# Top-32 attention with a feed-forward block: the mask as a parametric ReLU on ScalarE, the mean taken from x

## The chip, the cores and the metric

One core of a Trainium2 chip runs the whole program. The metric is the device time of one execution in microseconds (us); a comparison goes by the median of some runs. A core has TensorE (PE; its weight loads are PEld), VectorE (DVE), ScalarE (ACT), GpSimd (POOL) and SyncE (SP), each with a queue of its own that is worked off in order. Waits between them go by semaphores.

## The reference

Inputs are q, k and v of 8 batches x 8 heads x 576 rows x 64, a gain of 512, and two weight matrices of 512 x 2048 and 2048 x 512 in float64.

```python
scores = scale * np.matmul(q, k.transpose(0, 1, 3, 2))
kth = np.partition(scores, -32, axis=-1)[..., -32:-31]
scores = np.where(scores >= kth, scores, -1e9)
scores = scores - np.max(scores, axis=-1, keepdims=True)
attn = np.exp(scores); attn = attn / (attn.sum(-1, keepdims=True) + 1e-09)
out = np.matmul(attn, v)                       # then (B,H,S,D) -> x of (B,S,H*D)
mu, var = mean(x), variance(x)                 # along a row of 512
xn = (x - mu) / np.sqrt(var + 1e-06) * g_ln
y = x + np.maximum(xn @ w_ch1, 0.0) @ w_ch2
```

So each row of scores keeps its 32 largest, and the result goes through a normalisation, a two-layer feed-forward and a sum.

## The kernel before, in words

**Units.** Attention is cut into 160 units. A whole unit is 128 query rows of a pair of heads (two tiles of 128 x 576 scores); a rest unit (32 of them) holds the last 64 rows of both heads in one tile. A job is a batch, a pair of heads and two or three units; a group is what shares one product with v. Batch 0 has jobs [0, 1], [2, 3] and the rests apart.

**Steps.** The program is written out by hand, in steps n. `scores` of unit n+1 (L345: matmuls, and copies from PSUM by ACT) and `select` of unit n (L379: four rounds of MAX8 with three MATCH_REPLACE8 a tile, on VectorE, that find the 32nd largest value `thr` and the largest, `top`) stand in step n. In step n+1 POOL masks (`prepare`, `mask`, L398 and L412): it writes -1e30 where a score is below `thr` and adds the scores. In step n+2 ACT takes the exponentials (`weigh`, L422) with their sum, and TensorE turns them (`turn`, L441). In step n+3, after a group's last unit, `values` multiplies by v and `place` turns the result back and writes it to x, divided by the sums (`put`, L518). Sums of a group are inverted by `reciprocal` on VectorE. For the first 16 units (`shared`) ACT does half of the mask, with Sign and Relu, and POOL subtracts.

**Weights.** The float64 weights come in 32 pieces of 128 x 512 (`Piece`), two a step, batches 0 to 15. `fetch` loads a piece a step ahead; `split` takes size, low word and sign apart on ACT (Abs, Copy, Sign; L170 to L174) and limits the size on POOL (L175); a step later `shift` moves its bits on VectorE (L178) and `join` adds and signs it on POOL (L184, L185). For w_ch1, once four pieces of a column block are there, `mean_of` has TensorE take the mean over rows, weighted with the gain (L216), and `centre` on VectorE multiplies by the gain and subtracts (L227). So the mean of x never has to be taken from x.

**Feed-forward.** `Block` (L555) holds two or three row tiles of x. `stats` gives mean and variance on VectorE (L569), `std` the square root on ACT (L573), `inverse` the reciprocal. `items` lists its TensorE work with costs: `turn_x`, `hidden` (matmul with w1, then Relu on ACT, L619) and `project` (matmul with w2; at the end ACT scales with `rstd`, L633, POOL adds x, L634, and SP stores). `give` puts a block's items on the list `todo` at a step that is counted from its last unit (L709). `fill` stands eight times in a step and takes items off the list, as many as the planner's share allows: 1.2 us a call while weights are not all there, later an eighth of VectorE's planned cost of the unit (10.3 or 5.3 us) less TensorE's own (`slot`, L766). An item with a condition (`may`) holds up those behind it: `hidden` needs its columns centred, `project` its piece joined, the last one the block's `inverse`.

**Buffers.** Scores have 4 buffers, exponentials 3, raw weights and x share 4, PSUM has 5 of a short kind and 3 for products.

Of the kernel before, what the change touches and what calls it, by code (L numbers as in the profile page):

```python
# [18 lines left out]
MASKED = -1.0e30  # L19
LN_EPS = 1.0e-6  # L20
J = 4
# [7 lines left out]
def kernel(  # L29
# [9 lines left out]
):  # L39

# [48 lines left out]
    scpool = pool("sc", 4)  # L89
    wpool = pool("wk", 2)  # L90
    epool = pool("e", 3)
# [40 lines left out]
    class Piece:  # L132
# [26 lines left out]
        def split(self):  # L159
            def tmp(name, dt):  # L160
                return hpool.tile([P, DM], dt, tag="h", name=name)

            high = self.raw[:, :, 1].bitcast(FP32)
            self.size = tmp("size", U32)
            self.low = tmp("low", FP32)

            pl, tag = ((opool, "o"), (rpool, "r"))[self.i % 2]
            self.sign = pl.tile([P, DM], FP32, tag=tag, name="sign")
            size_f = self.size[:].bitcast(FP32)
            nc.scalar.activation(size_f, high, AF.Abs)  # L170
            nc.scalar.activation(
                self.low[:], self.raw[:, :, 0], AF.Copy, bias=2.0, scale=2.0**-51
            )
            nc.scalar.activation(self.sign[:], high, AF.Sign)  # L174
            nc.gpsimd.tensor_scalar(size_f, size_f, HIGH_MAX, HIGH_MIN, ALU.min, ALU.max)  # L175
# [6 lines left out]
        def join(self):  # L182
            size = self.size[:]
            nc.gpsimd.tensor_tensor(size, size, self.low[:].bitcast(U32), ALU.add)  # L184
            nc.gpsimd.tensor_tensor(  # L185
                self.dst, size.bitcast(FP32), self.sign[:], ALU.mult
            )
            ready[self.i] = now[0]
# [4 lines left out]
    centred = [None] * (DFF // DM)  # L193
    pieces = [Piece(i) for i in range(2 * NF)]
    gmat = [None]
    means = {}

    grow = hpool.tile([NC, P], FP32, tag="h", name="grow")

    def load_gain():  # L200
        ps = turned()
        nc.tensor.transpose(ps[:, 0:NC], grow[:], ident[0:NC, 0:NC])
        nc.scalar.copy(gcol[:], ps[:, 0:NC])
        ones = hpool.tile([P, P], FP32, tag="h", name="ones")
        nc.gpsimd.memset(ones[:], 1.0)
        gmat[0] = hpool.tile([P, NC, P], FP32, tag="h", name="gmat")
        for c in range(NC):
            nc.gpsimd.tensor_scalar(
                gmat[0][:, c], ones[:], gcol[:, c : c + 1], 1.0 / DM, ALU.mult, ALU.mult
            )  # L210

    def mean_of(nb):

        means[nb] = product("mean")
        for c in range(NC):
            nc.tensor.matmul(  # L216
                means[nb][:],
                gmat[0][:, c],
                w1[:, c, nb * DM : (nb + 1) * DM],
                start=(c == 0),  # L220
                stop=(c == NC - 1),
            )

    def centre(nb):
        for c in range(NC):
            w = w1[:, c, nb * DM : (nb + 1) * DM]
            nc.vector.scalar_tensor_tensor(  # L227
                out=w, in0=w, scalar=gcol[:, c : c + 1], in1=means[nb][:],
                op0=ALU.mult, op1=ALU.subtract,
            )  # L230
        centred[nb] = now[0]
# [4 lines left out]
    for n in range(-1, 2 * NF):  # L236
        size = 0 if n < 0 else 2
        batches[n], queue = queue[:size], queue[size:]

    def weights(n, phase):  # L240

        now, before = batches.get(n, []), batches.get(n - 1, [])
        if phase == 0:
            for x in batches.get(n + 1, []):
                x.fetch()
            for x in before:
                x.shift()
            for x in now[0::2]:
                x.split()
        elif phase == 1:  # L250
            for x in before:
                x.join()
            for x in now[1::2]:
                x.split()
            for x in batches.get(n - 2, []):
                if x.i < NF and x.c == NC - 1:
                    mean_of(x.i // NC)
        elif phase == 2:
            for nb in means:
                if centred[nb] is None:  # L260
                    centre(nb)
# [67 lines left out]
    class Unit:  # L329
        def __init__(self, job, group, qt):  # L330
            self.job, self.group, self.qt = job, group, qt
            self.rest = qt == J
            self.tiles = [(0, 1)] if self.rest else [(0,), (1,)]
            self.shared = False
# [63 lines left out]
    def prepare(u):  # L398

        nt = len(u.tiles)  # L400
        u.bias = small.tile([P, 2], FP32, tag="bias", name="bias")
        u.e = epool.tile([P, 2, S], FP32, tag="e", name="e")
        if u.shared:
            u.less = small.tile([P, 1], FP32, tag="less", name="less")
            nc.scalar.mul(u.less[:], u.thr[:, 0, 7:8], -1.0)
            nc.scalar.mul(u.bias[:, 0:nt], u.top[:, 0:nt, 0], -scale)
            nc.scalar.activation(u.e[:, 0], u.sc[:, 0], AF.Sign, bias=u.less[:])
            nc.scalar.activation(u.e[:, 0], u.e[:, 0], AF.Relu, scale=MASKED)
        else:
            nc.gpsimd.tensor_scalar_mul(u.bias[:, 0:nt], u.top[:, 0:nt, 0], -scale)  # L410

    def mask(u, t):  # L412
        e, sc = u.e[:, t], u.sc[:, t]
        if u.shared and t == 0:
            nc.gpsimd.tensor_tensor(e, sc, e, ALU.subtract)
        else:
            nc.gpsimd.tensor_scalar(  # L417
                e, sc, u.thr[:, t, 7:8], MASKED, ALU.is_lt, ALU.mult
            )
            nc.gpsimd.tensor_tensor(e, e, sc, ALU.add)  # L420

    def weigh(u, t):  # L422
        g = u.group
        if g.den is None:
# [3 lines left out]
            u.e[:, t], u.e[:, t], AF.Exp, bias=u.bias[:, t : t + 1], scale=scale,  # L428
# [126 lines left out]
    class Block:  # L555
# [7 lines left out]
        def stats(self, i):  # L563
# [6 lines left out]
            nc.vector.bn_aggr(out=self.mv[:, i, :], in_=st[:])  # L570

# [10 lines left out]
        def items(self):  # L582
# [38 lines left out]
            def project(i, f):  # L621
# [9 lines left out]
                if f == NF - 1:  # L631
                    o = opool.tile([P, DM], FP32, tag="o", name="o")
                    nc.scalar.mul(o[:], ps["o"][:], self.rstd[:, i : i + 1])  # L633
                    nc.gpsimd.tensor_tensor(o[:], o[:], self.x[i], ALU.add)  # L634
                    for dst, rows in self.dsts[i]:
                        nc.sync.dma_start(dst, o[rows, :])
# [9 lines left out]
                        lambda f=f: done(centred[f * P // DM]),  # L646
# [45 lines left out]
    for u in units[: max(n for n in batches if batches[n]) + 1]:  # L692
        u.shared = True

# [11 lines left out]
    for j in jobs:  # L706
        if j.hp == NHP - 1:
            b = j.b
            step = j.last + 4  # L709
# [24 lines left out]
    for j in fresh[2:]:  # L734
# [6 lines left out]
    def pe_cost(n):  # L741
# [3 lines left out]
        if at(n - 2):  # L745
            c += 0.67 if at(n - 2).rest else 1.0
        u = at(n - 3)
        if u and u.group.last == n - 3:
            c += 3.0
# [22 lines left out]
    recips, rows_of = {}, {}  # L772

    def arrived(n, key, x):
        blk, i = block_of[key]
        blk.x[i] = x
        rows_of.setdefault(n + 1, []).append((blk, i))

    load(fresh[0], nc.sync, nc.scalar)
    weights(-1, 0)  # L780
    turn_heads(fresh[0])
    load(fresh[1], nc.sync, nc.scalar)
    nc.sync.dma_start(grow[:], g_ln.rearrange("(c p) -> c p", p=P))
    scores(units[0])
    turn_heads(fresh[1])
    load(fresh[2], nc.sync, nc.sync)
    for n in range(END):
# [4 lines left out]
        u, nxt, mk, ex = at(n), at(n + 1), at(n - 1), at(n - 2)  # L792
        g = at(n - 3).group if at(n - 3) and at(n - 3).group.last == n - 3 else None
        g = g if g and not g.quick else None
        late = at(n - 4)
# [3 lines left out]
        if ex:  # L799
            weigh(ex, 0)  # L800
        if nxt:
            scores(nxt)
        if n == 0:
            load_gain()
# [6 lines left out]
        if mk:  # L811

            prepare(mk)
            order = list(range(len(mk.tiles)))
            if mk.shared:
                order.reverse()
            mask(mk, order[0])
        weights(n, 0)
        fill()
# [3 lines left out]
        if parts:  # L823
            parts[0]()
        if ex and ex.rest:
            keep_den(ex)
# [7 lines left out]
        for blk, i in rows_of.pop(n, []):  # L834
            blk.stats(i)
        for blk in gives.get(n - 1, []):
            blk.std()
        if mk and len(mk.tiles) > 1:
            mask(mk, order[1])
        weights(n, 1)  # L840
        fill()
# [3 lines left out]
        if late:  # L845
            place_rest(late.job.b, late.job.hp)
        fill()
# [6 lines left out]
        if ex and ex.group.last == n - 2 and ex.group.sums is not None:  # L854
            recips.setdefault(n + 1, []).append(ex.group.sums)
        last_rest = at(n - 3)
# [4 lines left out]
        weights(n, 2)  # L861
# [3 lines left out]
        fill()  # L865
        if mk and mk.job.last == n - 1:
            load_values(mk.job)
        if ex and ex.group.quick and ex.group.last == n - 2:

            g = ex.group  # L870
            values(g)
            for den in recips.pop(n + 1):
                nc.vector.reciprocal(den, den)
            place(g)
        if u:
            select(u, 3)
        if g and g.job.hp == NHP - 1:
            for qt in g.qts:
                if qt < J:
                    arrived(n, (g.job.b, qt), xs[g.job.b, qt])  # L880
        if late and late.job.hp == NHP - 1:
            r = late.job.b // 2
            arrived(n, ("r", r), rs[r])
# [34 lines left out]
```

## Time and profile before

| | us |
|---|---|
| median of 3 runs | 1763.67 (1763.66 to 1764.48) |
| profiled execution | 1762.83 |
| its span, first to last instruction | 1760.9 |
| PE busy | 1651.3 (94%) |
| DVE busy | 1522.1 (86%) |
| POOL busy | 1196.2 (68%) |
| ACT busy | 983.8 (56%) |
| DMA | 66.7 MB, 38 GB/s on the mean |

Busy time is that of an engine in the span of the profiled execution. Matmuls overlap, and their ends are modelled, so a busy TensorE is judged by the distance of the starts. A group's row gives line, engine, operation, written and read tiles, shapes and count, then its busy time and the mean of one instruction in ns, then the idle time of the engine just before and who ended it. In the timeline a row is the start, the duration, and what ran; brackets hold the idle time before it.

### The profile page before, as it was taken

Reading aid. Unit: us, or ns where it says so; the run is one execution under the profiler, and the core shown is the slowest. Engines: PE = TensorE matmul, PEld = TensorE weight load, DVE = VectorE, ACT = ScalarE, POOL = GpSimd, SP = SyncE. Lnnn points to the kernel's source line nnn. Section 1 sums busy time; section 2 is a strip of 40 time slices with the busy share of each in tenths; the row PEclk is TensorE's granted clock in tenths of the full one; section 3 lists DMA queues with packets and bytes.
Section 4 is the critical chain, followed back from the end, with each engine's and each line's share of the span. In section 5 each row is a group of like instructions: output and inputs, shape, how many; then the busy total and the mean of one; then the engine's idle time right before and its main releaser. Section 6 shows DMA issues by size and latency. Waiting matters only on the chain.

```text
span 1760.9 us, 23686 instructions
## 1 busy us (share of the span) xinstructions
PE 1651.3 (94%) x7433; PEld 1005.2 (57%) x7433; DVE 1522.1 (86%) x3160; ACT 983.8 (56%) x2621; POOL 1196.2 (68%) x882
## 2 busy tenths in 40 slices
PE   3668879999899999999999999999999999999998
PEld 1335446666555575655546666575555757575564
DVE  7998779999999999999999999999999999960000
ACT  5676856565655566557646656566555665561110
POOL 5886887777776787777777687687768868760000
PEclk9868899999999999999999999999999999999999
DMA  5432312101210022002111121012201210000000
GB/s 136 124 86 67 90 37 54 40 20 21 50 31 7 26 47 47 20 20 47 21 42 25 21 53 28 26 24 45 39 12 26 43 34 20 20 20 12 0 18 12
DMA packets 249348, 66.70 MB, mean 38 GB/s; under 512 B 240516, under 2 KB 240520, under 8 KB 249224
## 3 DMA queue, kind: packets, MB, share of 16 engines
q1 hardware_dynamic: 244488, 64.61, 16.2%
q10 hardware_dynamic: 4736, 0.59, 0.3%
q8 instruction: 59, 0.97, 0.2%
q14 instruction: 65, 0.53, 0.1%
HBM read 55.71 MB, written 9.44 MB: 37 GB/s over the span
## 4 chain that ended last, share of the span: by engine, by line
PE 45%; DVE 33%; issue 14%; POOL 5%; ACT 2%; DMA 1%; DVEq 0%; POOLq 0%; SPq 0%; ACTq 0%
DVE m L387 17%; PE hps L607 15%; PE ops L624 14%; DVE wk L392 13%; PE scps L370 6%; PE tp L451 4%; PE av L504 4%; POOL e L417 2%; PE av L511 1%; DVE size L178 1%; POOL e L420 1%; DVE qT L325 1%; DVE kT L325 1%; DVE w L227 1%; ACT e L427 1%
## 5 line engine op out<-in xcount | busy, mean ns | idle before, releaser
L417 POOL TENSOR_SCALAR e<-sc,m 128x576 f32<-128x576 f32 x272 | 604.1, 2221 | 208.9 <-DVE m L387 137.9
L387 DVE MAX8 m<-wk 128x8 f32<-128x576 f32 x864 | 612.6, 746 | 3.7
L607 PE MATMUL hps<-xT,w 128*128 128x256 f32 (+1 forms) x2048 | 545.0, 411 | 7.4 <-ACT xT L599 6.2
L624 PE MATMUL ops<-w,h 128*128 128x512 f32 x1152 | 542.2, 601 | 7.1 <-POOL w L185 7.1
L607 PEld LDWEIGHTS hps<-xT,w 128*128 128x128 f32 x2048 | 374.0, 191 | 113.7 <-issue 18.8
L392 DVE MATCH_REPLACE8 wk<-m,wk 128x576 f32<-128x576 f32 x576 | 423.8, 742 | 0.0
L420 POOL TENSOR_TENSOR e<-e,sc 128x576 f32<-128x576 f32 x272 | 383.4, 1410 | 22.7
L624 PEld LDWEIGHTS ops<-w,h 128*128 128x128 f32 x1152 | 202.6, 191 | 195.5 <-issue 180.4
L370 PE MATMUL scps<-kT,qT 64*128 64x288 f32 (+3 forms) x1344 | 236.4, 439 | 26.5 <-DVE qT L325 19.9
L351 ACT COPY sc<-scps 128x288 f32<-128x288 f32 x576 | 198.5, 417 | 91.4 <-PE scps L370 83.1
L451 PE MATMUL tp<-ident,e 128*128 128x128 f32 x1152 | 180.9, 281 | 56.1 <-ACT e L427 56.0
L427 ACT ACTIVATE e<-e,bias 128x576 f32<-128x576 f32 x288 | 227.4, 790 | 8.6 <-POOL e L420 4.0
L451 PEld LDWEIGHTS tp<-ident,e 128*128 128x128 f32 x1152 | 143.8, 144 | 144.8 <-ACT e L427 70.9
L370 PEld LDWEIGHTS scps<-kT,qT 64*128 64x128 f32 (+1 forms) x1344 | 134.6, 181 | 136.1 <-issue 49.1
L392 DVE MATCH_REPLACE8 wk<-m,sc 128x576 f32<-128x576 f32 x288 | 211.9, 742 | 0.0
L387 DVE MAX8 m<-sc 128x8 f32<-128x576 f32 x288 | 203.4, 743 | 9.2 <-ACT sc L351 9.1
L619 ACT ACTIVATE h<-hps 128x256 f32<-128x256 f32 (+1 forms) x256 | 104.8, 412 | 185.9 <-PE hps L607 185.0
L634 POOL TENSOR_TENSOR o<-o,x 128x512 f32<-128x512 f32 x32 | 40.7, 1271 | 245.8 <-ACT o L633 224.9
L463 ACT COPY pt<-tp 128x512 f32<-128x512 f32 x256 | 150.3, 587 | 90.0 <-PE tp L451 88.4
L504 PE MATMUL av<-pt,vb 128*64 128x256 f32 (+2 forms) x1088 | 146.0, 409 | 2.8 <-ACT pt L463 2.0
L504 PEld LDWEIGHTS av<-pt,vb 128*64 128x64 f32 x1088 | 72.5, 140 | 68.6 <-issue 24.5
L516 ACT COPY oT<-av 128x256 f32<-128x256 f32 (+2 forms) x68 | 26.2, 386 | 108.7 <-PE av L511 108.7
(71 smaller groups left out, 1038.6 us busy)
## 6 DMA issues: line engine op xcount, KB each, us to landing
vb<-in_v_dram SPq DMA_DIRECT2D x136, 128.0 KB, 2.4
raw<-in_moe_w_ch_dram SPq DMA_DIRECT2D x32, 512.0 KB, 4.2
kin<-in_k_dram SPq DMA_DIRECT2D x128, 72.0 KB, 2.4
qin<-in_q_dram SPq DMA_DIRECT2D x120, 72.0 KB, 2.5
out_dram<-o SPq DMA_DIRECT2D x32, 256.0 KB, 2.1
ends<-in_v_dram SPq DMA_DIRECT2D x136, 16.0 KB, 2.1
dr<-den SPq DMA_DIRECT2D x64, 0.2 KB, 1.7
out_dram<-o SPq DMA_DIRECT2D x8, 128.0 KB, 2.3
```

The source lines that it names most:

```text
L351: nc.scalar.copy(u.sc[:, t, s * HALF : (s + 1) * HALF], made[s][t][:, 0:HALF])
L370: nc.tensor.matmul(ps[i * R : i * R + ql, o : o + width], qT[r, q0 : q0 + ql], kT[r, k0 : k0 + width], start=True, stop=True,)
L387: nc.vector.max(m[:, t, :], u.cur[t])
L392: nc.vector.match_replace(u.wk[t][:], m[:, t, :], u.cur[t], LOWEST)
L417: nc.gpsimd.tensor_scalar(e, sc, u.thr[:, t, 7:8], MASKED, ALU.is_lt, ALU.mult)
L420: nc.gpsimd.tensor_tensor(e, e, sc, ALU.add)
L427: nc.scalar.activation(u.e[:, t], u.e[:, t], AF.Exp, bias=u.bias[:, t : t + 1], scale=scale, accum_out=g.den[:, col : col + 1],)
L451: nc.tensor.transpose(ps[:, c * P : (c + 1) * P], u.e[:, t, c * P + t * R : (c + 1) * P + t * R], ident[:],)
L463: nc.scalar.copy(g.pt[:, t * J : (t + 1) * J, q0 : q0 + P], ps[:].rearrange("p (c n) -> p c n", n=P),)
L504: nc.tensor.matmul(av[h * D : (h + 1) * D, 0 : g.nq], vb[:, h * J + c, :], g.pt[:, h * J + c, 0 : g.nq], start=(c == 0), stop=False,)
L607: nc.tensor.matmul(ps["h"][:, 0:N], w1[:, c, f * P : (f + 1) * P], xT[0][:, c, 0:N], start=(c == 0), stop=(c == NC - 1),)
L624: nc.tensor.matmul(ps["o"][:], hT[f][:, i * P : (i + 1) * P], w2[:, f, :], start=(f == 0), stop=(f == NF - 1),)
```

## The change

The mask is no longer made on POOL. ACT takes Prelu of `thr - score` with a slope of 2**-90: negative or zero (the kept scores) is scaled to almost nothing, positive stays. Exp then takes a scale of -scale * 2**90 and a bias of scale * (thr - top), which POOL computes for the unit; so kept scores give their exponential and the others zero. Both stand in `weigh`, one step after the selection; a unit's turning, values, placing and its block come a step earlier, too, and buffers of scores and exponentials fall to 3 and 2. The gain is multiplied in `join` on POOL; `mean_of` and `centre` go, and POOL subtracts the mean from x after `stats`, which now stands at the end of the step that placed x. The conversion of the output (Identity with a scale and a bias) adds the mean again. Odd pieces get their size by a product with the sign on POOL in place of Abs. Weights start a step earlier, the second job's k and q are turned in step 0, and a copy in front loads ACT's table.

```diff
-MASKED = -1.0e30
+SLOPE = 2.0**-90
-    scpool = pool("sc", 4)
+    scpool = pool("sc", 3)
-    epool = pool("e", 3)
+    epool = pool("e", 2)
             size_f = self.size[:].bitcast(FP32)
-            nc.scalar.activation(size_f, high, AF.Abs)
+            if self.i % 2 == 0:
+                nc.scalar.activation(size_f, high, AF.Abs)
...
+            if self.i % 2:
+                nc.gpsimd.tensor_tensor(size_f, high, self.sign[:], ALU.mult)
...
+            size = size.bitcast(FP32)
+            if self.i < NF:
+                nc.gpsimd.tensor_scalar_mul(size, size, gcol[:, self.c : self.c + 1])
+            nc.gpsimd.tensor_tensor(self.dst, size, self.sign[:], ALU.mult)
...
-    for n in range(-1, 2 * NF):
-        size = 0 if n < 0 else 2
-        batches[n], queue = queue[:size], queue[size:]
+    for n in range(-1, NF - 1):
+        batches[n], queue = queue[:2], queue[2:]
...
+        b = u.bias[:, 0:nt]
+        nc.gpsimd.tensor_tensor(b, u.thr[:, 0:nt, 7], u.top[:, 0:nt, 0], ALU.subtract)
+        nc.gpsimd.tensor_scalar_mul(b, b, scale)
-    def mask(u, t):
...
         nc.scalar.activation(
-            u.e[:, t], u.e[:, t], AF.Exp, bias=u.bias[:, t : t + 1], scale=scale,
+            u.e[:, t], u.sc[:, t], AF.Prelu, bias=u.thr[:, t, 7:8], scale=-1.0, alpha=SLOPE
+        )
+        nc.scalar.activation(
+            u.e[:, t], u.e[:, t], AF.Exp, bias=u.bias[:, t : t + 1], scale=-scale / SLOPE,
             accum_out=g.den[:, col : col + 1],
...
             nc.vector.bn_aggr(out=self.mv[:, i, :], in_=st[:])
+            nc.gpsimd.tensor_scalar_sub(x, x, self.mv[:, i, 0:1])
...
-                    nc.scalar.mul(o[:], ps["o"][:], self.rstd[:, i : i + 1])
+                    nc.scalar.activation(
+                        o[:], ps["o"][:], AF.Identity,
+                        bias=self.mv[:, i, 0:1], scale=self.rstd[:, i : i + 1],
+                    )
...
-                        lambda f=f: done(centred[f * P // DM]),
+                        lambda f=f, c=c: done(ready[f * P // DM * NC + c]),
...
-            step = j.last + 4
+            step = j.last + 3
...
-    for j in fresh[2:]:
+    for j in fresh[1:]:
...
     load(fresh[0], nc.sync, nc.scalar)
+    nc.scalar.copy(gcol[:, 0:1], eps[:])
+    for x in batches[-1]:
+        x.fetch()
+    turn_heads(fresh[0])
+    nc.sync.dma_start(grow[:], g_ln.rearrange("(c p) -> c p", p=P))
+    load(fresh[1], nc.sync, nc.scalar)
+    scores(units[0])
+    load_gain()
     weights(-1, 0)
-    turn_heads(fresh[0])
-    load(fresh[1], nc.sync, nc.scalar)
-    nc.sync.dma_start(grow[:], g_ln.rearrange("(c p) -> c p", p=P))
-    scores(units[0])
-    turn_heads(fresh[1])
-    load(fresh[2], nc.sync, nc.sync)
+    weights(-1, 1)
...
-        u, nxt, mk, ex = at(n), at(n + 1), at(n - 1), at(n - 2)
+        u, nxt, ex = at(n), at(n + 1), at(n - 1)
-        if ex:
-            weigh(ex, 0)
         if nxt:
             scores(nxt)
...
+        if ex:
+            prepare(ex)
         weights(n, 0)
+        if ex:
+            weigh(ex, 0)
         fill()
         if ex and len(ex.tiles) > 1:
             weigh(ex, 1)
         fill()
-        if parts:
-            parts[0]()
         if u:
             select(u, 1)
...
-        for blk, i in rows_of.pop(n, []):
-            blk.stats(i)
...
     def arrived(key, x):
         blk, i = block_of[key]
         blk.x[i] = x
+        blk.stats(i)
...
         weights(n, 1)
-        fill()
+        if parts:
+            parts[0]()
+        if ex and ex.rest:
+            keep_den(ex)
         fill()
         if g:
             place(g)
...
         if u:
             select(u, 3)
-        if g and g.job.hp == NHP - 1:
+        for x in (g, quick):
+            if x and x.job.hp == NHP - 1:
...
+                        arrived((x.job.b, qt), xs[x.job.b, qt])
```

## The prediction

> **What bounds the kernel now.** I read the slices first, then sums over stretches, then the groups with shapes apart, the waits, and single stretches of the timeline. Two lines of the slices:
>
> ```profile
> PE   3668879999899999999999999999999999999998
> DVE  7998779999999999999999999999999999960000
> PEclk9868899999999999999999999999999999999999
> ```
>
> One slice is 44 us. TensorE is full from about the seventh slice on; VectorE is full until four slices before the end. The last four are TensorE alone. The sums over stretches (columns: stretch and its length; busy time of PE, PEld, DVE, ACT, POOL with counts; granted clock; DMA):
>
> ```profile
> 0.00:150.00 150.00, 80.73 (x290) 44.98 (x291) 138.01 (x258) 97.06 (x237) 113.23 (x102) 0.84 0.43 109
> 150.00:290.00 140.00, 121.25 (x603) 77.35 (x602) 116.40 (x239) 94.93 (x243) 107.22 (x86) 0.91 0.25 64
> 505.00:1568.00 1063.00, 1054.32 (x4944) 644.45 (x4943) 1051.45 (x2212) 630.70 (x1714) 797.69 (x569) 1.00 0.15 31
> 1568.00:1761.00 193.00, 187.25 (x618) 108.56 (x616) 2.78 (x9) 34.72 (x81) 16.07 (x11) 1.00 0.03 10
> ```
>
> From 505 us to the end TensorE lacks 9 + 6 us; the matmul starts there stand at the pitches that the forms have elsewhere (216 ns for 128x256, 429 ns for 128x512), so it doesn't wait. VectorE lacks 12 us of 1063. Both are full, and neither waits for POOL or ACT. Time is lost only before: in the first 290 us TensorE lacks 88 us and runs at a clock of 0.84 and 0.91, since its feed-forward work starts at 149.7 us (first row of `hps`). I call D(n) the start of unit n's first MAX8 on `sc`: D(0) 14.8, D(9) 129.1, D(10) 143.6, D(20) 261.0, D(52) 553.7, D(159) 1559.0. What VectorE waits for is in its waits:
>
> ```profile
> DVE den L810 <- ACT den L439: 17.5, 3, 12.4
> DVE size L178 <- POOL size L175: 13.9, 5, 4.3
> DVE m L387 <- ACT sc L351: 9.1, 6, 3.4
> DVE st L569 <- ACT x L520: 7.1, 2, 6.9
> ```
>
> Of these, 22.6 us lie between 167 and 257 us (den 2.3 and 2.8, size 13.9, m 3.4, st 0.3). So the end is set by two things: when the weights and the first block let the feed-forward start, and the full stretch behind.
>
> **The mask leaves POOL, and costs the path nothing there.**
>
> ```profile
> L417 POOL TENSOR_SCALAR e<-sc,m 128x576 f32<-128x576 f32 x272 | 604.1, 2221 | 208.9 <-DVE m L387 137.9 <-ACT h L619 12.6 <-PE scps L370 8.2
> L420 POOL TENSOR_TENSOR e<-e,sc 128x576 f32<-128x576 f32 x272 | 383.4, 1410 | 22.7
> L407 ACT ACTIVATE e<-sc,less 128x576 f32<-128x576 f32 x16 | 12.4, 775 | 0.0
> L227 DVE SCALAR_TENSOR_TENSOR w<-w,gcol,mean 128x512 f32<-128x512 f32 x16 | 10.8, 734 | 0.0
> L208 POOL TENSOR_SCALAR gmat<-ones,gcol 128x128 f32<-128x128 f32 x4 | 1.4, 373 | 13.0 <-ACT gcol L203 13.0
> ```
>
> POOL loses 272 x 3.63 and 16 x 1.51 = 1012 us, of which from 505 us on nobody waits for any. ACT gains 288 Prelu. The trace has none; the nearest row is Sign with a column as bias, 775 ns (bounds 683 of Relu without one, 790 of Exp): 288 x 0.775 = 223 us, less 16 x (0.775 + 0.683 + 0.21 + 0.20) = 30 and 16 Abs x 0.67 = 11. ACT goes from 984 to 1166 us, from 59% to about 73% in the full stretch, and has no new table loads (32 stand in both instruction orders). Prelu and Exp together take 1.5 us a tile and stand in TensorE's order behind scores, values and two fills (1.2 + 1.9 + 1.6 us), so nothing is added to TensorE's path while that cover stays; if TensorE led VectorE so far that it isn't there, a step would show up to 1.5 us, 160 x 1.5 = 240 us at the very most.
>
> The Trainium skill speaks against this: "ScalarE: Activation LUTs", section Rules for kernel authors, would put max- and add-like work on VectorE, not ScalarE. Here VectorE is full (1051 of 1063 us); by that rule 288 more passes of 0.66 us would stand on its path and the sum would end 190 us later. The rows decide for ScalarE.
>
> **The centring leaves VectorE and TensorE.** 16 instructions with a pitch of 0.66 us go: 10.5 us of VectorE, all before unit 10, all on its path. 32 `mean` matmuls (14 us at the low clock) go from a TensorE that waits there anyway: nothing. POOL gets a product with `gcol` in 16 joins: bounds 0.66 us (L175, constants) and 1.97 (L417 x 512/576); I take 0.8, from the multiply by a column, L208: (373 - 233)/126 x 510 + 233 ns, 233 being L410's two elements. POOL's round in that stage is then 2 x (1.27 + 0.8 + 1.29) + 1.28 (sign product) + 2 x 0.66 + 0.5 (two small bias steps) = 9.8 us against VectorE's 11.7. At 1.97 it would be 12.2 and cost 0.5 us in each of 8 steps; at 0.66 nothing.
>
> **The shifts.** 32 shifts take 1.4 and 0.83 us where L420 is running, and 0.42 where POOL is still or in a one-input pass:
>
> ```profile
> 146.40 1.47 DVE L178 TENSOR_SCALAR size<-size 128x512 uint32<-128x512 uint32 x1
> ...
> 178.10 0.43 DVE L178 TENSOR_SCALAR size<-size 128x512 uint32<-128x512 uint32 x1 [4.32 <-POOL size L175]
> ```
>
> A pair costs 2.07 us now, at best 0.75. Without the mask POOL is often still when the shift comes; I take 1.3 to 1.6 a pair: 16 x 0.6 = 9 us, bounds 0 and 21. The page "GPSIMD Engine Reference", section Key points, says that POOL shares its SBUF interfaces with VectorE and contends with its two-port modes; taken alone, with POOL's mask gone, it would give all 21 and a time 12 us lower than mine. POOL's joins, two-input too, remain.
>
> **The start and the step earlier.** The first k and q are turned alone; VectorE no longer waits for the second pair before unit 0 (13.4 us, DMA `kin`), and the table load (9.99 us) moves ahead: D(0) falls from 14.8 to about 10.7. But the turn (1.36 us) and the first shift pair then stand in step 0, and the latter waits for POOL, by 2.6 us. Weights, exponentials and first block come a step earlier. So D(9) is 10.7 + 9 x 9.64 (a unit) + 9 x 1.5 (shifts) + 3 x 1.36 (turns) + 2.6 = 118, against 129.1, and the feed-forward, at D(9) + 6 in place of D(10) + 6, starts at 124 in place of 150. On SP the same loads stand; k and q of the third job move behind two weight fetches, which wait for POOL's sign product; they have two steps (24 us) for a landing of 2.5 us.
>
> From there to D(20): before 261.0 - 143.6 = 117.3, with the 22.6 us of waits. After, one whole unit more: +9.6; the waits shrink. POOL's chain from Abs to the second shift loses the 1.41 us of L415 but gets 1.28 and the bias; in the w2 half a step has 8.2 us of POOL in place of 11.7, so I drop the three waits of 1.7, half of the two of 4.3, and most of the 6.5 us near 250: 13 us (bounds 0 and 22.6). D(20) = 118 + 117.3 + 9.6 - 13 - 2 = 230, which is 31 us less. Bounds: everything as before 11 (centring, start), everything good 46. TensorE allows it: 86 us of work up to unit 20, 106 us there.
>
> **The full stretch.** Counted in the instruction orders, unit 52 is reached with 4.3 us more of feed-forward done, and behind the last exponentials the rows are the same: -3 us. New waits: x's statistics move from behind the second selection of the next step to the end of this one. TensorE lags there, and x is late:
>
> ```profile
> 582.72 1.40 DVE L387 MAX8 m<-sc 128x8 f32<-128x576 f32 x2
> ...
> 586.07 0.93 ACT L520 ACTIVATE x<-xo,den 128x64 f32<-128x64 f32 x4 [1.19 <-PE xo L543]
> ...
> 588.26 0.68 DVE L569 BATCH_NORM_STATS2 st<-x 128x6 f32<-128x512 f32 x1
> ```
>
> x ends 4.3 us after D(55), where the statistics would now stand; so at 11 of 16 arrivals (3.2 to 4.5). VectorE waits there, and the next selection is queued behind. I expect it to pay once, not each time: a VectorE that is later by 4 us makes TensorE lag less at the next arrival, and TensorE, which is as full, loses nothing. What is left is clipping: the lead of scores over selection varies by 6.5 us within a batch, and the exponentials a step sooner leave about 9.5 us. I take 1 us a batch, 8 in all (bounds 0 and 25). The 36 subtractions (0.8 us by L208's line, 1.97 at most) lie on POOL, which has some 80% of the full stretch free; the bias steps of the next unit are queued behind them, and so is that unit's Exp by 1 to 2 us, 16 times, under TensorE's two fills; without these it would be up to 32 us. The 36 conversions of the output with one column more (0.1 us, Sign's 775 less Relu's 683) have their next reader on SP alone: nothing. No gain at the end: TensorE has 185 us of work left there.
>
> **Sum.** Against the profiled execution's 1762.83 us (span 1760.9 and 1.93 around it; the median is 0.84 more): -31 - 3 + 8 = -26, so 1737 us, 1738 against the median; I say 1737.
>
> **The rivals.**
> 1. All bounds good: POOL quiet, waits gone, no clipping: -46 - 5: 1713. For it: 0.42 us shifts wherever POOL is still. Against: POOL's joins are 6.7 us a step.
> 2. The early gain mostly stays away: POOL's chain through Abs still ends last, gmul is dear: -11 - 3 + 8: 1757. For it: the waits of 4.3 us begin with Abs behind late scores, and Abs for even pieces stays.
> 3. Slower. The statistics wait at each arrival, 12 x 3.9 + 3 x 1.2 (rests) = 51 us: -31 - 3 + 51: 1781. For it: the rows above. Against: two full engines share one lag. It decides from 34/15 = 2.3 us an arrival.
> 4. Nothing measurable, the gains and clipping cancelling. VectorE and TensorE both already have their order fixed, so there is little for it.
>
> **How the numbers follow.** Forecast 0.54, rival 1 0.12, rival 2 0.16, rival 3 0.14, rival 4 0.04. The forecast's own range is 1722 to 1752. The range reaches from just under rival 1 to beyond rival 2, which leaves out rival 3: 1710 to 1768. A difference of under 0.2% (3.5 us) is about what this measurement can't tell from none. Faster: 0.54 + 0.12 + 0.16 = 0.82; same 0.04; slower 0.14.
>
> **What would show it.** First `hps` near 124 us; D(20) near 230; shifts under 0.8 us on average; ACT near 1166 us with Prelu near 0.78; TensorE still full from 300 us on, the last selection's end near 1543; waits of `st` for x under 10 us in all. Wrong if D(20) is above 248, if `st` waits over 2 us each time, or if TensorE waits for `e` by more than 2 us a batch.

## The result, and the profile after

| | us |
|---|---|
| before, median of 4 runs | 1763.93 (1763.66 to 1764.48) |
| changed, median of 4 runs | 1912.8 (1907.13 to 1918.42) |
| ratio, 95% interval | 1.0843 (1.080 to 1.0886) |
| changed, profiled execution and its span | 1907.13, 1905.4 |
| forecast | 1737, range 1710 to 1768 |

The changed kernel is 149 us slower, and the forecast had it 27 us faster. The side was wrong, and so was the range.

Busy time of the changed kernel, and three of its slices:

```profile
PE 1647.5 (86%) x7401; PEld 981.9 (52%) x7401; DVE 1506.1 (79%) x3144; ACT 1170.8 (61%) x2830; POOL 322.6 (17%) x561
...
PE   3568789888789888989889888989889989899998
...
DVE  7987899977887988888988988798989989790000
...
PEclk9679899999899999999999999999999999999999
```

TensorE and VectorE do as much work as before (1651 and 1522 us), but over a longer time: the unbroken rows of nines have become eights and nines in turn, and TensorE is full only in the last slices, where it works alone. The clock is near full speed from the tenth slice on, so it isn't the clock. The same full stretch as in the forecast, 505 to 1568 us (length; busy PE, PEld, DVE, ACT, POOL; clock; DMA):

```profile
505.00:1568.00 1063.00, 949.43 (x4361) 553.05 (x4357) 934.38 (x1956) 702.45 (x1705) 105.70 (x267) 0.99 0.14 28
```

TensorE lacks 114 us there (9 before) and VectorE 129 (12 before). The waits of the changed kernel say for what (us in total, times, longest):

```profile
PEld tp L408 <- ACT e L384: 336.1, 189, 7.5
PE tp L408 <- ACT e L384: 224.9, 169, 6.7
...
DVE st L526 <- ACT x L477: 90.3, 16, 8.1
...
DVE m L356 <- ACT sc L320: 84.2, 22, 5.9
```

Two candidates stand side by side: TensorE waits for the exponentials in nearly every step, and VectorE waits for x, then for scores. One whole step from the timeline of the changed kernel, PE, then ACT, then DVE (start, duration; in brackets the idle time before):

```profile
1012.46 1.24 PE L339 MATMUL scps<-kT,qT 64*128 64x288 f32 x8
1013.63 2.37 PE L461 MATMUL av<-pt,vb 128*64 128x320 f32 x16
1015.94 0.81 PE L468 MATMUL av<-pt,ends 128*128 128x320 f32 x2
1016.58 1.03 PE L565 MATMUL hps<-xT,w 128*128 128x256 f32 x4
1018.88 0.65 PE L408 MATMUL tp<-ident,e 128*128 128x128 f32 x4 [1.27 <-ACT e L384]
...
1013.25 1.49 ACT L320 COPY sc<-scps 128x288 f32<-128x288 f32 x4 [1.14 <-PE scps L339]
1016.78 0.43 ACT L473 COPY oT<-av 128x320 f32<-128x320 f32 x1 [2.04 <-PE av L468]
1017.10 0.78 ACT L381 ACTIVATE e<-sc,m 128x576 f32<-128x576 f32 x1
1017.96 0.77 ACT L384 ACTIVATE e<-e,bias 128x576 f32<-128x576 f32 x1
...
1021.59 0.69 DVE L526 BATCH_NORM_STATS2 st<-x 128x6 f32<-128x512 f32 x1 [6.66 <-ACT x L477]
```

Read it by ACT. Its queue holds the copy of the next scores, the copy of oT, and then Prelu. ACT is idle for 2.04 us with the threshold long there, because the copy of oT stands ahead and waits for TensorE's values. Only when these are done come Prelu and Exp, 1.5 us; TensorE has one short run of fills (four `hps` matmuls, 1.03 us) for that time and then stands for 1.27 us. So TensorE waits for ACT, which waited for TensorE, in one step. In the kernel before, the exponential came ahead of the scores:

```profile
951.75 0.77 ACT L427 ACTIVATE e<-e,bias 128x576 f32<-128x576 f32 x1
...
953.44 1.49 ACT L351 COPY sc<-scps 128x288 f32<-128x288 f32 x4 [0.84 <-PE scps L370]
```

Of 288 Prelu in the changed kernel, 84 start right behind a copy of scores and 61 behind a copy of oT; none waited for VectorE's threshold.

### The profile page after: what moved, and what is told of

It reads as the page before. It is cut to its first block, busy times and chain, and to the rows that moved or that the text cites. A ratio compares the mean times of both kernels' runs of the same rounds, so it can differ in the third digit from the quotient of the medians.

```text
span 1905.4 us, 23371 instructions
## 1 busy us (share of the span) xinstructions
PE 1647.5 (86%) x7401; PEld 981.9 (52%) x7401; DVE 1506.1 (79%) x3144; ACT 1170.8 (61%) x2830; POOL 322.6 (17%) x561
## 3 DMA queue, kind: packets, MB, share of 16 engines
q1 hardware_dynamic: 244488, 64.61, 15.1%
## 5 line engine op out<-in xcount | busy, mean ns | idle before, releaser
L565 PE MATMUL hps<-xT,w 128*128 128x256 f32 (+1 forms) x2048 | 560.6, 414 | 4.7 <-ACT xT L557 4.7
L582 PE MATMUL ops<-w,h 128*128 128x512 f32 x1152 | 548.2, 601 | 0.0
L408 PE MATMUL tp<-ident,e 128*128 128x128 f32 x1152 | 195.6, 295 | 225.3 <-ACT e L384 224.9
L408 PEld LDWEIGHTS tp<-ident,e 128*128 128x128 f32 x1152 | 137.5, 148 | 369.8 <-ACT e L384 336.1
L320 ACT COPY sc<-scps 128x288 f32<-128x288 f32 x576 | 204.7, 405 | 154.1 <-PE scps L339 134.8
L384 ACT ACTIVATE e<-e,bias 128x576 f32<-128x576 f32 x288 | 223.3, 775 | 30.4 <-POOL bias L374 13.6
L339 PE MATMUL scps<-kT,qT 64*128 64x288 f32 (+3 forms) x1344 | 216.1, 440 | 18.6 <-DVE qT L295 16.5
L381 ACT ACTIVATE e<-sc,m 128x576 f32<-128x576 f32 x288 | 223.6, 777 | 0.0
L339 PEld LDWEIGHTS scps<-kT,qT 64*128 64x128 f32 (+1 forms) x1344 | 124.2, 185 | 125.3 <-issue 54.3
L373 POOL TENSOR_TENSOR bias<-m,m 128x2 f32<-128x2 f32 (+1 forms) x160 | 31.7, 198 | 633.6 <-DVE m L356 624.3
L595 POOL TENSOR_TENSOR o<-o,x 128x512 f32<-128x512 f32 x32 | 40.7, 1271 | 458.6 <-ACT o L591 458.6
```

What stands on the lines that cost most here:

```text
L320: nc.scalar.copy(u.sc[:, t, s * HALF : (s + 1) * HALF], made[s][t][:, 0:HALF])
L339: nc.tensor.matmul(ps[i * R : i * R + ql, o : o + width], qT[r, q0 : q0 + ql], kT[r, k0 : k0 + width], start=True, stop=True,)
L381: nc.scalar.activation(u.e[:, t], u.sc[:, t], AF.Prelu, bias=u.thr[:, t, 7:8], scale=-1.0, alpha=SLOPE)
L384: nc.scalar.activation(u.e[:, t], u.e[:, t], AF.Exp, bias=u.bias[:, t : t + 1], scale=-scale / SLOPE, accum_out=g.den[:, col : col + 1],)
L408: nc.tensor.transpose(ps[:, c * P : (c + 1) * P], u.e[:, t, c * P + t * R : (c + 1) * P + t * R], ident[:],)
L565: nc.tensor.matmul(ps["h"][:, 0:N], w1[:, c, f * P : (f + 1) * P], xT[0][:, c, 0:N], start=(c == 0), stop=(c == NC - 1),)
```

## The experiments

Theory A: ScalarE's order. The first exponential of a step stands behind copies of what TensorE makes in that same step, and TensorE waits for it. Theory B: the statistics, now at the end of the step, hold VectorE, and all the rest follows. Theory C: one step is too short a distance from threshold to exponential. Runs 1, 2, 4, 5, 6 and 11 are one execution each; the four of the changed kernel lie within 11.3 us, so differences of that size are not read from them.

**1 and 2: mend one, then the other.** The first run, `e1_exp_first`, moves the exponential only:

```diff
+        if ex:
+            prepare(ex)
+            weigh(ex, 0)
         if nxt:
             scores(nxt)
...
-        if ex:
-            prepare(ex)
         weights(n, 0)
-        if ex:
-            weigh(ex, 0)
```

> The changed kernel, but the bias, Prelu and Exp of a unit's first tile stand before the copies of the next scores on ScalarE, as the exponentials did in the kernel before. Theory A (ScalarE's order: in the changed kernel Prelu and Exp stand behind score copies and oT copies that wait for TensorE in the same step, so TensorE's transposes wait 1.3 us in nearly each step, 225 us in all): these waits fall under 70 us and the time to 1760 to 1800 us. Theory B (x's statistics at the end of the step hold VectorE, 90 us, and what follows is late): the waits of the transposes stay over 170 us and the time over 1870. Theory C (a step less between selection and exponentials, the threshold comes too late): Prelu now waits for VectorE, and the time stays over 1870.

Measured: 1791.79 us, 121 less than the changed kernel and inside theory A's band; TensorE's waits for the exponentials fell from 225 to 110 us, and not under 70. The second run, `e2_stats_later`, leaves the order and moves the statistics back behind the second selection of the next step:

```diff
-        blk.stats(i)
+        rows_of.setdefault(now[0] + 1, []).append((blk, i))
...
+        for blk, i in rows_of.pop(n, []):
+            blk.stats(i)
         for blk in gives.get(n - 1, []):
             blk.std()
```

> The changed kernel, but the statistics of x stand where they stood before, behind the second selection of the next step. Theory A: VectorE's 90 us of waiting for x go, but TensorE's waits for e stay near 225 us and the time between 1880 and 1915 us. Theory B: the time falls to 1800 to 1830. Theory C: over 1880.

Measured: 1911.78 us, no difference. Its waits:

```profile
PE tp L408 <- ACT e L384: 219.6, 167, 6.7
...
DVE m L356 <- ACT sc L320: 116.4, 33, 7.8
...
DVE den L768 <- ACT den L396: 38.2, 22, 12.2
DVE st L526 <- ACT x L477: 31.5, 13, 6.5
```

The wait of `st` fell from 90 to 32 us, and waits for scores and for `den` rose by 32 and 23. VectorE had only to wait for TensorE somewhere; the line that shows it is not its cause. Theory B falls as the cause of the 149 us.

**3: both.** `e3_both` holds both edits.

> Both edits, Prelu and Exp of the first tile first on ScalarE, and the statistics a step later. Theory A: with the waits of every step gone, what was forecast for the early stage shows: 1725 to 1755 us, under the kernel before. Theories B and C: B 1790 to 1830, C over 1870.

Measured: 1753.68 us (1751.65 to 1754.33), ratio to before 0.9943 (0.9926 to 0.9959). With the order mended the statistics cost 38 us (1791.79 less 1753.68); without that, nothing. The two waits are not a sum.

**4: a step more of distance.** `e4_step_later` puts exponentials two and values three steps behind, with buffers 4 and 3 as before, and keeps the changed order in the step:

```diff
-        u, nxt, ex = at(n), at(n + 1), at(n - 1)
+        u, nxt, ex = at(n), at(n + 1), at(n - 2)
```

> The changed kernel, but masking, exponentials, turning, values and blocks stand a step later, as in the kernel before (4 and 3 buffers of scores and exponentials); on ScalarE Prelu and Exp still stand behind the score copies of their step. Theory A: the order on ScalarE is the same, so the transposes still wait about 1.3 us a step and the time stays between 1870 and 1930 us. Theory C: with a step more the threshold is early enough: 1740 to 1780.

Measured: 1952.8 us, outside both expectations. Theory C falls: a threshold that is a step older helps nothing while Prelu queues behind the copies. Why it got 40 us slower still is taken up with the seventh and eleventh runs.

**5: the order alone, in the kernel before.** `e5_before_exp_behind` keeps the masks on GpSimd, the two steps and the statistics:

```diff
-        if ex:
-            weigh(ex, 0)
         if nxt:
             scores(nxt)
...
         weights(n, 0)
+        if ex:
+            weigh(ex, 0)
         fill()
```

> The kernel before, with one thing changed: the first exponential of a step is issued behind the score copies, the copy of oT and the first phase of the weights, where the changed kernel has it; masks on GpSimd, two steps of distance and the statistics stay as they were. Theory A (ScalarE's order): copies 1.5 us and Exp 0.8 us now follow TensorE's scores, against a cover of two fills of 0.8 to 1.0 us each; TensorE waits 0.3 to 0.8 us in each of 160 steps, 50 to 130 us: 1810 to 1890 us. Rival (the place is harmless by itself; it hurts only with a Prelu in front or with a distance of one step): 1764 to 1775 us.

Measured: 1831.1 us, 67 more than before. Here nothing of the change is in but the place of two lines of code. In its timeline TensorE waits at the same matmul, by less, as there is no Prelu:

```profile
1034.34 1.95 PE L504 MATMUL av<-pt,vb 128*64 128x256 f32 x16
1036.22 0.70 PE L511 MATMUL av<-pt,ends 128*128 128x256 f32 x2
1036.75 1.02 PE L624 MATMUL ops<-w,h 128*128 128x512 f32 x2
1038.14 0.66 PE L451 MATMUL tp<-ident,e 128*128 128x128 f32 x4 [0.37 <-ACT e L427]
```

**6: more cover.** `e6_cover` is the changed kernel with `parts[0]()` and `keep_den` moved behind two more fills.

> The changed kernel with the first transposes of e two fills later in TensorE's order, nothing else moved. Theory A: the wait of 1.3 us a step is what Prelu and Exp stick out behind the two fills; two more of 0.8 to 1.0 us cover it, and the changed kernel's 1912.8 falls by 80 to 140 us, to 1770 to 1830 us (what the statistics at the end of the step cost, 38 us between the first and the third run, may then be seen). Rival (the wait only moves on, to the later transposes of the step or to the values of the next): 1880 to 1915 us.

Measured: 1807.96 us, 105 less. The order of Prelu, Exp and the copies of scores and oT on ScalarE is untouched; the fills in front of the waiting matmul were doubled (where a group ends, its placing stands in front of it, too).

**What TensorE waits, against what the units take.** D(n) is the start of unit n's first MAX8 on the scores, as in the prediction. From the timelines of the profiled executions, for units 50 to 150: the time between D(50) and D(150), and the idle time of TensorE in front of transposes of e in it.

| run | D(50) to D(150), us | TensorE waits for e, us | difference |
|---|---|---|---|
| before | 936.2 | 6.6 | 929.6 |
| changed | 1049.3 | 110.7 | 938.6 |
| 1, exponential first | 950.2 | 29.3 | 920.9 |
| 2, statistics later | 1052.5 | 110.5 | 942.0 |
| 3, both | 931.0 | 19.0 | 912.0 |
| 5, before with exponential behind | 978.6 | 42.3 | 936.3 |
| 6, more cover | 975.1 | 47.4 | 927.7 |

The changed kernel loses 113 us here and waits 104 us more for e; the fifth run loses 42 and waits 36 more; the sixth loses 39 and waits 41 more. The rest of the 144.5 us by which its span is longer than before: -13 up to D(20), +35 from there to D(50), +10 behind D(150).

**7 and 11: what a step sooner is worth.** `e7_two_steps_first` is the fourth run with both edits of the third.

> Parametric ReLU on ScalarE with the old distance: exponentials two steps behind the scores and first in ScalarE's step, statistics behind the second selection of the next step, the rest as changed. In the third run ScalarE waited 69 us for the bias and 35 us for the threshold, most of it early. Theory A, with the step sooner worth little or nothing: no such waits, the early stage as fast as in the changed kernel (first hps near 130 us): 1732 to 1750 us. Rival (the step sooner is itself a gain, as the forecast had it): 1758 to 1775 us.

Measured: 1794.86 us (1792.42 to 1797.75), ratio 1.0175 (1.016 to 1.019). It missed both expectations: the step sooner is worth 41 us against the third run. The timeline shows one place:

```profile
889.70 2.37 PE L461 MATMUL av<-pt,vb 128*64 128x320 f32 x16
892.00 0.81 PE L468 MATMUL av<-pt,ends 128*128 128x320 f32 x2
892.65 0.60 PE L408 MATMUL tp<-ident,e 128*128 128x128 f32 x4
893.33 0.44 PE L500 MATMUL xo<-ident,oT 128*128 128x128 f32 x2
894.90 0.66 PE L408 MATMUL tp<-ident,e 128*128 128x128 f32 x4 [1.14 <-ACT e L384]
```

There is no fill between the values and the second transposes. With values three steps behind their group they fall on the short step of a unit with one tile (4.9 us of VectorE), in which the shares of the fills are zero, and the second tile's Prelu and Exp lie bare: from the start of the second `xo` to the transposes 1.41 us pass, 1.14 of them idle, at 22 places between 500 and 1500 us. Before, at the same 22 places and without Prelu, it was 0.60 us. With values two steps behind, the third run shows none. Against the kernel before this explains most of what is lost between D(50) and D(150): 20 places with 0.8 us more each, 16 of 22 us (958.1 against 936.2). Against the third run (931.0) it doesn't explain the 27 us alone: the third run waits for e at other places, so that TensorE's idle time in front of transposes of e is 23.8 us here and 19.0 there, 5 more. Another 12 us lie in the score matmuls: in 20 steps they take 1.43 us from the first start to the last in place of 0.84, in the kernel before too. Why they do, and where the rest lies, is not shown. `e11_two_steps_late_first` repeats this with the early stage of the eighth run, below:

> The eighth run's kernel with the old distance of two steps between scores and exponentials, and values three behind; order in the step, statistics and early stage as in the eighth run. What a step sooner is worth, with the early stage equal: in the seventh run TensorE stood 1.4 us behind the placing of 22 batches, in the steps of the short last unit, where values, transposes and no fill come together, 27 us between units 50 and 150. If this is all: 1738.7 + 30 to 45, 1768 to 1784 us. Rival (the seventh run lost its time early, behind the bias): 1737 to 1750 us.

Measured: 1784.92 us, 46 more than the eighth run, a microsecond beyond the expected band. D(50) to D(150) takes 958.2 us against 931.1. By its size the lost step fits the fourth run, too: 1912.8 and 41 to 46 give 1954 to 1959, and 1952.8 was measured. That is a sum of two costs measured apart, not an experiment of its own.

**8: the exponential first only when the weights are done.** In the third run the first `hps` came at 150 us, against 130 in the changed kernel. Its waits of ACT in the first 150 us:

```profile
ACT e L384 <- POOL bias L374: 44.0, 8, 6.1
```

Early in the kernel GpSimd is busy with weights, and the bias of the exponentials is queued behind them; an Exp at the head of ACT's step waits for it by up to 6.1 us, and holds the score copies. So `e8_first_when_late` takes the third run's order from step 18 on, and the changed kernel's before:

```diff
+        if ex and n >= LATE:
+            prepare(ex)
+            weigh(ex, 0)
         if nxt:
             scores(nxt)
...
-        if ex:
+        if ex and n < LATE:
             prepare(ex)
```

> The third run's kernel with the exponentials first in the step only from step 18 on, when the weights are done; before that the changed kernel's order. In the third run the first hps came at 150 us against 130 in the changed kernel, and unit 20 at 260 against 248. If the early gain is kept to the end: 1753.7 less 12 to 18, 1735 to 1743 us. Rival (TensorE or its clock gives it back later): 1749 to 1756 us.

Measured: 1738.73 us (1737.13 to 1741.16), ratio 0.9861 (0.9845 to 0.9878). The early gain stays to the end. In its timeline ACT does Prelu and Exp while TensorE makes the scores, and the copy follows:

```profile
861.12 0.78 ACT L381 ACTIVATE e<-sc,m 128x576 f32<-128x576 f32 x1
861.99 0.78 ACT L384 ACTIVATE e<-e,bias 128x576 f32<-128x576 f32 x1
862.67 0.19 ACT L384 ACTIVATION_READ_ACCUMULATOR e<-e,bias 128x1 f32 x1
862.89 0.20 ACT L396 ACTIVATE den<-den 128x1 f32<-128x1 f32 x1
863.00 1.28 ACT L320 COPY sc<-scps 128x288 f32<-128x288 f32 x4
```

**9 and 10: the early stage.** `e9_split_first` splits `weights(n, 0)`: the even piece's conversion (Abs, low, Sign and the clip) goes ahead of the scores, fetches and shifts stay.

```diff
+        weights(n, -1)
         if ex and n >= LATE:
             prepare(ex)
             weigh(ex, 0)
```

> The eighth run's kernel, with the even piece's conversion (Abs, low, Sign on ScalarE and the clip on GpSimd) issued first in the step, ahead of the score copies. In the eighth run GpSimd's clip waited 40 us for Abs and the shift 23 us for the clip, with Abs queued behind copies that wait for TensorE; the forecast had dropped 13 us of such waits. If this place of Abs is why unit 20 came at 244 to 248 us and not at 230: D(20) falls by 10 to 15 us and 1738.7 to 1724 to 1731 us. Rival (the next in line, the odd piece or the joins, takes the wait over): 1735 to 1741 us.

Measured: 1730.72 us (1729.98 to 1731.54), ratio 0.9814 (0.9801 to 0.9828), the fastest kernel of this study; D(20) 235.8 against 243.9. The time is at the upper end of the expected band, D(20) fell by 8 and not by 10 to 15. Of the 7.4 us between D(9) and D(20) (124.4 to 117.0), by the timelines, shorter shifts make 2.9 (14 in 6.9 us in place of 9.8), waits for `den` and x 2.6, and waits of shifts for the clip only 1.7 (17.7 to 16.0). So the place of Abs is worth 8 us, but not in the way expected: the wait for the clip was mostly taken over, as the rival said. `e10_no_gain_product` is the eighth run without the 16 products.

> The eighth run's kernel without the 16 products with the gain on GpSimd (their work is left out, so the first weights aren't scaled by g). The product was taken at 0.8 us and measured 1.57; the prediction said GpSimd's round then stays near VectorE's and the excess costs up to 0.5 us in each of 8 steps. By that: unit 9 up to 4 us sooner, 1734 to 1739 us. Rival (GpSimd's round sets the steps with first weights): 16 x 1.57 = 25 us less at most, 1714 to 1728 us.

Measured: 1730.95 us (1730.68 to 1732.47), 7.8 less than the eighth run; D(9) 111.1 against 119.6. Between the two expectations: the products cost 8 us in all, and not 4 at most. Up to D(9) the 18 shifts take 7.8 us in place of 12.2, and VectorE waits 2.3 us for the clip in place of 5.3: with less work on GpSimd, VectorE's shifts are shorter, too.

## Why the prediction was wrong, by its steps

**The step that failed: the cover of Prelu and Exp.** The prediction said that they "stand in TensorE's order behind scores, values and two fills (1.2 + 1.9 + 1.6 us), so nothing is added to TensorE's path while that cover stays". It counted the cover on TensorE's queue alone. On ACT's queue the diff puts them behind the copies of these same scores and values, so scores and values are no cover: the exponential can't start before they are done. What is left are the fills, 1.0 us in the step shown, against 0.43 (copy of oT) + 0.78 + 0.77 us. The prediction's own upper bound, 1.5 us a step and 240 at most, named the size, but tied it to a TensorE that leads; it was given no chance. Its own mark of being wrong came: between D(50) and D(150), five batches of units, TensorE waited 110.7 us for `e`, 22 us a batch, where the mark was 2. The fifth run shows the price of the place alone (67 us), the sixth that cover pays it back (105 us), the first that the place does (121 us).

The Trainium skill has the rule, in "PSUM — Partial Sum Buffer", section Engine vs sequencer instructions: the queues of ScalarE, VectorE and GpSimdE are strict first-in, first-out. The changed kernel's rows agree: ACT stood idle for 2.04 us ahead of the copy at 1016.78 with a Prelu behind it that needed nothing from TensorE.

**Sizes and engine of the mask: right.** Prelu 777 ns (taken 775), ACT 1170.8 us (forecast 1166). ACT has room for the mask once order and distance are right: in the eighth run units 50 to 150 take 931.1 us with it, before 936.2 without. With the old distance (eleventh run) it is 958.2: there the mask does lie on the path, in the steps without fills.

**Statistics at the end of the step: the mechanism was nearer to rival 3's.** The forecast had VectorE pay once and 8 us in all; rival 3 had 51. With the order mended, it is 38 us (first against third run). The sentence that failed is "I expect it to pay once, not each time": 16 waits of 5.6 us in the changed kernel, 10 of 2.6 in the first run. Even without the failed step the changed kernel would have stood near 1777 us (worked out, not run: 1791.79 less the 15 of the early order, third less eighth run), close to rival 3's 1781, and slower than before. In the changed kernel itself, moving them is worth nothing, as the second run shows.

**A step sooner in the full stretch.** The prediction took -3 us from counts of fills. Units 50 to 150 gain 5 us between before and the third run. That the old distance would have cost 41 to 46 us with Prelu it didn't see. In part this is the step on which the values fall, where it had not looked; the rest stays open, as said with the seventh run.

**The early stage.**

```profile
L381 ACT ACTIVATE e<-sc,m 128x576 f32<-128x576 f32 x288 | 223.6, 777 | 0.0
...
L528 POOL TENSOR_SCALAR x<-x,mv 128x512 f32<-128x512 f32 x32 | 49.9, 1568 | 126.9 <-DVE mv L527 89.2 <-PE hps L565 34.3 <-ACT sc L320 3.3
...
L195 POOL TENSOR_SCALAR size<-size,gcol 128x512 f32<-128x512 f32 x16 | 25.1, 1567 | 1.7
...
L186 DVE TENSOR_SCALAR size<-size 128x512 uint32<-128x512 uint32 x32 | 20.4, 646 | 20.4 <-POOL size L183 20.4
```

These are groups of the changed kernel. The shifts: 646 ns, a pair 1.29 us, just under the 1.3 to 1.6 taken. By the Trainium skill's "GPSIMD Engine Reference", section Key points, taken alone (GpSimd contends with VectorE's two-port modes, and its mask is gone), a pair would have taken 0.75, an estimate from the prediction's best pair. D(0) 11.6 (10.7 forecast). D(9) 124.2 against 118; in the second and eighth runs, with the statistics later, 118.8 and 119.6, so that step held but for a wait of `st`. First `hps` 129.7 (124 forecast, 149.7 before). D(20) 247.7 against 230, just inside the mark of 248 above which it said it would be wrong. Two terms failed. The waits that it had fall by 13 us, 9 of them waits of shifts for the clip, stayed in the main: the clip's are 20.4 us in the changed kernel, 15.1 of them between D(9) and D(20), and 13.9 before. GpSimd itself waits there for ACT, whose Abs is queued behind score copies. The ninth run moves it. GpSimd's waits between 118 and 245 us, first in the eighth run and then in the ninth:

```profile
POOL size L183 <- ACT size L176: 27.4, 6, 6.3
...
POOL size L182 <- ACT sign L180: 7.3, 3, 4.1
```

```profile
POOL size L182 <- ACT sign L180: 14.3, 6, 4.9
POOL size L183 <- ACT size L176: 13.7, 5, 3.9
```

The wait for Abs halves and the one for the odd piece's sign doubles; what would end it wasn't tried and is open. The product with `gcol` was taken at 0.8 us by L208's line with a fixed part; it measures 1.57, between the bounds of 0.66 and 1.97, and costs 8 us in place of nothing. The size alone doesn't explain that: put into the prediction's own sum, 1.57 makes GpSimd's round 11.4 us, still under VectorE's 11.7. The price lay beside the round, as the tenth run shows: of 8.5 us up to D(9), shifts are 4.4 and waits for the clip 3.0. Rival 2 had named both, and 11 us for all that is left of the early gain; D(20) came 13 us sooner. In the full stretch no instruction waited for the 36 subtractions themselves (1.57, taken 0.8), as it said; at the first block TensorE did, 2.8 us in all at 125.2 and 126.8 us.

**The sum.** The eighth run changes the place of two items in the step and otherwise keeps all of the change: it stands at 1738.73, against a forecast of 1737. That they are so near is luck. In the profiled executions D(20) came 17 us sooner (243.9 against 261.0) and not 31; from D(20) to the end of the span 8.5 us were gained (1491.4 against 1499.9), where the forecast had a loss of 5. The two misses, 14 us each, cancel. And that the path on which the terms were put stayed a path was not examined.

## What to carry to other kernels

Cover must be counted on every queue that the work passes. When an instruction is moved on an in-order engine, list what now stands ahead of it, what that waits for, and whether it is the very work that was to hide it. Two engines that hand work to each other in a step show idle time on both, and a large wait may be the echo: move one thing at a time and see which row's loss only changes its name.

## What the runs showed of the hardware that was not expected

On GpSimd a tensor-scalar operation with a column of scalars takes 1567 ns for 128x512 in fp32 (L195, L528), with two constants 627 ns (L183), and two tensors 1271 to 1308 ns (L595, L182): one input and a column is slower than two inputs. The kernel before had the hint: its 128x128 product with a column, 373 ns, was scaled by its elements with a fixed part taken from a two-element row. In proportion it would have been 1.49 us. And on VectorE the same shift takes from 0.42 us with GpSimd still (changed kernel, at 14.41 us) to 1.45 us (at 184.90 us, with two products on GpSimd beside it); without the gain's products the 18 shifts up to D(9) took 4.4 us less in all.
